# Transposed planes joined behind a later gate in every Strassen pair, and the third row's weight sums loaded sooner through a larger ring

## The chip, the cores and the metric

The kernel runs on one core of a Trainium2 chip. The metric is the device time of one execution in microseconds (us). The engines of the core are TensorE (PE in the profile), VectorE (DVE), ScalarE (ACT) and GpSimd (POOL); SyncE (SP) issues all transfers, in order.

## The reference

Eight heads of banded attention over 8 batches of 576 positions, then a gated feed-forward layer over the 4608 tokens, in float32.

```python
rel = pos[:, None] - pos[None, :]
mask = (rel >= 0) & (rel < 64)
scores = np.where(mask, scale * q @ k.T, -1e9)
attn = softmax(scores);  x = attn @ v          # 4608 x 512 after the heads are joined
gate = 1.0 / (1.0 + np.exp(-(x @ w_gate)))     # 512 -> 1536
val = x @ w_val
return (gate * val @ w_out).astype(np.float32) # 1536 -> 512
```

## The kernel before

The 4608 tokens are 12 tiles of 384. Every float32 product of the feed-forward layer is three matmuls: each operand is split into a high part, cast to fp32r on ACT, and the rest, a subtraction on DVE.

Tiles 0 and 1 go through the layer plainly (`up`, `down`). Tiles 2 to 11 go in five pairs, s = 1 to 5, each as a two by two block product by the Strassen-Winograd scheme, with seven block products instead of eight. A pair has 6 values of k, each with 7 products for the gate (m = 0) and 7 for the value (m = 1); these are the matmuls `pr` of L668. Then it has 7 times 6 last products, the matmuls `y`, also of L668. A "step" below is one pair of `pr` products, or one last product. The products of a k give, in turn, `u` and `c` (sums on DVE), `g` (tanh on ACT, L450) and `h` (DVE, L455), and `h` is summed (L621 to L643) and split (L750, L751) for the last products.

Pairs 2 to 5 use weight blocks and sums of blocks (`wd`, `wod`) that pair 1's phase puts into DRAM. For the up projections POOL makes the sums S1 to S4 (`sums_make`, L589 to L595) from the plain float32 weights: `sums_load` brings two rows `a` of `w32d` for each k and m, POOL makes the sums `sw`, and `sums_split` splits them into the weights `ws` of pair 1 (L602 on ACT, L604 on DVE for m = 1, L609 on POOL for m = 0). The rows `a` of k = 0 have tiles of their own, those of k = 1 share one tile of the ring `raw` (6 buffers of 4 KB a partition), those of k = 2 and later take two buffers of the ring `w32` (3 buffers of 2 KB a partition). The ring `w32` also holds `yo` (outputs of tiles 0 and 1 on their way to DRAM), `t1` (a sum of x blocks) and planes `pl`, below. DVE makes the sums of the down weights from `wa` (`wo_sums`, L553 to L561).

The attention of a pair is done while the pair before it is in the layer. For each unit (tile t, pair of heads p) PE makes the scores, DVE and ACT the exponentials `p` (two halves, h = 0 and 1), then `p` must be transposed before it meets `v`. Units before tile 4, and some of tiles 4 and 5, are transposed by PE (`stage_b`: `pp`, L347, and a copy on ACT, L352). The others go by the transfers: `stage_d` copies `p` on ACT into two 16-bit planes `pl` (L368), and SP issues a transposing transfer into `plT` (L374); `stage_e` joins the planes back into `p` on ACT (L383). Then PE makes the outputs (`outputs`, L406), and ACT copies them to `xf`, from which DVE makes the next pair's x sums.

The order on the engines comes from a list of events with a time each (`put`), sorted, and then from a scheduler of the framework that orders every engine but PE by a simulation; PE keeps the written order. `visit(("u", i), stage, ...)` places an attention stage behind step i of the up products, `visit(("d", i), ...)` behind last product i. In each pair three visits (v = 1 to 3 at steps u = 5, 19, 33) take two units each, c and d. `tc.issue_after(marks["gate"])` puts an instruction behind the latest tanh `g`, `marks["cast"]` behind the latest cast of L750, and `chain[-1]` behind the latest exponential.

SP's transfers use eight semaphores in turn, so a transfer also waits until the one eight places earlier has landed. In the orders below `DMAHW`*n* is that semaphore.

Of the kernel before, what the change touches and what calls it, by code (L numbers as in the profile page):

```python
# [27 lines left out]
def attn_ffn(ctx: ExitStack, tc: tile.TileContext, qT, kT, vN, w_gate, w_val, w_out, out, outT):  # L28
# [18 lines left out]
    RAW, W32 = 6, 3  # L47
# [4 lines left out]
    mp = ctx.enter_context(tc.tile_pool(name="mp", bufs=2))  # L52
# [30 lines left out]
    marks = {"pT": {}}  # L83
    chain = []
# [273 lines left out]
    def stage_d(t, p, last, home=None, base=6):  # L358


        for h in range(2):
            halves = st[(t, p, h)].rearrange("p u c -> p (u c)").bitcast(U16).rearrange("p (n e) -> p e n", e=2)
            pool, tag, bufs = home or ((mp, "g", 4) if last else (mp, "w32", W32))
            if tag[0] == "e":
                tag = f"e{EXTRA - 2 + h}"
            pl = pool.tile([P, 2, TT], U16, name=f"pl{h}_{t}_{p}", tag=tag, bufs=bufs)
            with tc.issue_after(marks["cast"]) if last and not home else nullcontext():
                nc.scalar.copy(pl, halves)  # L368
            if last:
                plT = ap.tile([P, 2 * UP, P], U16, name=f"plT{h}_{t}_{p}", tag=last, bufs=2)  # L370
            else:
                ft, fp = unit(t // 2, base + h)
                plT = xp.tile([P, 2 * UP, P], U16, name=f"plT{h}_{t}_{p}", tag=f"xf{4 * (ft % 2) + fp}")
            nc.sync.dma_start_transpose(out=plT, in_=pl.rearrange("p e n -> p (e n)"))  # L374
            turned_of[(t, p, h)] = plT

    def stage_e(t, p, last=False):
        for h in range(2):
            halves = st[(t, p, h)].rearrange("p u c -> p (u c)").bitcast(U16).rearrange("p (n e) -> p n e", e=2)
            plT = turned_of.pop((t, p, h))  # L380
            mark = chain[-1] if t < 6 else marks["cast"] if last else marks["gate"] if h else None
            with tc.issue_after(mark) if mark else nullcontext():
                nc.scalar.copy(halves, plT.rearrange("p (e u) c -> p (u c) e", e=2))  # L383

    turned_of = {}
# [182 lines left out]
    def sums_load(m, k):  # L568
        aa = []
        for i in range(2):  # L570
            if (m, k) in EARLY:
                a = xp.tile([P, DM], F32, name=f"a{i}_{m}_{k}", tag=f"x{EARLY[m, k] + i}")
            elif k == 1:
                if i == 0:
                    both = mp.tile([P, 2, DM], F32, name=f"a_{m}_{k}", tag="raw", bufs=RAW)
                a = both[:, i, :]
            else:
                a = mp.tile([P, DM], F32, name=f"a{i}_{m}_{k}", tag="w32", bufs=W32)
            nc.sync.dma_start(out=a, in_=w32d[m][k + i * NK])
            aa.append(a)  # L580
        sums[m, k] = aa
# [208 lines left out]
    def put(tm, o, f, *a):  # L790
        events.append((tm, o, f, a))

    AHEAD = 2
    DPT = DNT / TB
    APT = (0.9, 0.8, 0.9, 1.5, 0, 2.7, 0, 0, 1.6)
    stages = (stage_a, stage_b, stage_c, stage_s, stage_n, stage_v, stage_d, stage_e, stage_o)
    LOAD_AHEAD = 8
    BEFORE, BEHIND = 0, 12
# [9 lines left out]
    for n in range(2 * NP):  # L808
        t, p = divmod(n, NP)
# [6 lines left out]
    def unit(s, n):  # L816
        return 2 * s + n // 2 % 2, n // 4 + n % 2 * 2
# [9 lines left out]
    at, now = {}, 0.0  # L827
    MERGED = (0, 1, 2, 3)
    for n, (x, y, z) in enumerate(((4.5, 7.5, 8.5), (9, 12, 13), (13.5, 16, 17), (17.5, 20.5, 22), (22.5, 25, 26), (26.5, 30, 31), (31.5, 35, 36), (36.5, 40, 41))):
        u = unit(1, n)  # L830
# [20 lines left out]
    for i, (kind, t, j) in enumerate(plan):  # L851
        attend(i)
        at[(kind, t, j)] = now
        if (kind, t, j) == ("up", 0, 0):
            now = -9.9 - UPT / 2
# [10 lines left out]
        if (kind, t, j) == ("up", 0, 0):  # L866
            now = 0.0
    for i in range(KINDS * NF):
        j, m = divmod(i, KINDS)
# [37 lines left out]
        put(now + load, 7, wo_sums_load, k)  # L907
        put(now + make, 7, wo_sums, k)
    DOUBLE = (5, 19, 33)
    LAST_OUT, FIRST_IN = 6, 9  # L910
    for s in range(1, NS):
        fill.clear()

        def visit(key, *what):
            fill.setdefault(key, []).append(what)

        if s + 1 < NS:
            for v, u in enumerate(DOUBLE, 1):
                c, d = new = [unit(s + 1, 2 * v + i) for i in range(2)]
                visit(("u", u), 5, new, [unit(s + 1, 2 * v - 2 + i) for i in range(2)])  # L920
                visit(("u", u + 1.5), 4, *d)
                visit(("u", u + 2.5), 4, *c)
                home = (xp, "e", 1) if s == 1 and v < 3 else None
                visit(("u", u + 2.5), 6, *d, None, home)
                visit(("u", u + 6), 7, *d)
                if s == 1 and v < 3:
                    visit(("u", u + 7), 1, *c)
                elif s == 1 and v == 3:
                    visit(("u", u + 6), 1, *c)
                elif v < 3:  # L930
                    visit(("u", u + 4.5), 6, *c, None, home, 4)
                    visit(("u", u + 8.5), 7, *c)
                else:
                    visit(("u", u + 4.5), 6, *c, "k", (mp, "w32", W32))
                    visit(("d", 1), 7, *c, True)
            if s + 2 == NS:
                visit(("d", LAST_OUT), 8, c, d)
        if 1 <= s < NS - 2:
# [9 lines left out]
        for k in range(NK):  # L948
            if s == 1:
                for m in range(2):  # L950
                    make = (-28 + 7 * m, -29 + 6 * m)[k] if k < 2 else -25 + 8 * m
                    put(now + make - 6, 7, sums_load, m, k)
                    put(now + make, 7, sums_make, m, k)
                    for i, at_cut in zip((0, 2), (-14 + 2 * m, -10 + 2 * m) if k == 0 else (-13 + 1.5 * m, -5 + 1.5 * m)):
                        put(now + at_cut, 7, sums_split, m, k, i)
                        put(now + at_cut + 4, 7, sums_store, m, k, i)
                for n, d in ((0, -23 if k == 0 else -14), (4, -12 if k == 0 else -4), (5, -9 if k == 0 else -1)):
                    put(now + d, 7.5, w_load, s, k, n)
            else:
                for n in range(NPR):  # L960
                    put(now - 22 + 2.1 * n, 7.5, w_load, s, k, n)
            for n in range(NPR):
                for m in range(2):
                    put(now, 9, product, s, k, n, m)
                    now += PRT
                    if m == 0:
                        attend(("u", NPR * k + n - 0.5))
                attend(("u", NPR * k + n))
            put(now + 0.5, 5, h_prep, s, k)
            if k < EXTRA:  # L970
                put(now + 3, 5.1, h_early, s, k)
# [46 lines left out]
    for tm, _, f, a in events:  # L1018
        if f in (conv_a, conv_b, conv_c):
            with ExitStack() as behind:  # L1020
# [4 lines left out]
                j, m = divmod(a[0], KINDS)  # L1025
# [56 lines left out]
```

## Time and profile before

| | |
|---|---|
| three runs | 927.86, 931.34, 931.66 us, median 931.34 |
| profiled execution | 930.14 us, span 928.4 us |
| PE busy | 909.9 us, 98% of the span, 7002 matmuls |
| DVE, ACT, POOL busy | 711.2 (77%), 552.4 (59%), 154.2 (17%) us |
| TensorE clock granted | 1.00 over the span |

The span reaches from the first instruction to the last; the time of the execution is 1.7 us longer. PE is busy nearly everywhere, so the time moves only by what makes PE wait, or no longer wait.

### The profile page before, as it was taken

The numbers are of one execution on the slowest core, as the hardware profiler recorded it, in microseconds if no ns is written. First come the engines' busy times: TensorE is split into PE (matmuls) and PEld (weight loads), VectorE is DVE, ScalarE is ACT, GpSimd is POOL, SyncE is SP. The second block draws the span as 40 slices with busy tenths as digits, with TensorE's granted clock in tenths as the row PEclk, the third lists the DMA queues.
The fourth block names the chain that finished last, engine by engine and source line by source line (L and its number), as shares of the span: only waits on it lengthen the run. The fifth ranks groups of instructions, "written<-read, shape, count | busy, mean of one in ns | idle before, by whom it ended". The sixth has DMA issues, their size and how long they took to land.

```text
span 928.4 us, 20123 instructions
## 1 busy us (share of the span) xinstructions
PE 909.9 (98%) x7002; PEld 878.1 (95%) x7002; DVE 711.2 (77%) x1919; ACT 552.4 (59%) x1414; POOL 154.2 (17%) x232
## 2 busy tenths in 40 slices
PE   6999999999999999999999999999999999999998
PEld 4799999889999999999999999999999999999998
DVE  7999989889788995676896666897566797566882
ACT  7866766566565774653975545886446575222450
POOL 4210103803766010110110101100101100000000
PEclk9999999999999999999999999999999999999999
DMA  9899988989999999999989999989999898988374
GB/s 335 309 390 367 357 306 294 347 281 362 342 351 357 370 348 388 312 308 288 297 272 353 319 306 319 253 314 306 370 288 324 244 275 282 288 254 260 117 227 160
DMA packets 148710, 284.07 MB, mean 306 GB/s; under 512 B 54656, under 2 KB 76800, under 8 KB 148608
## 3 DMA queue, kind: packets, MB, share of 16 engines
q1 hardware_dynamic: 148608, 282.78, 92.3%
q8 instruction: 56, 0.92, 0.4%
q14 instruction: 46, 0.38, 0.1%
HBM read 220.20 MB, written 51.90 MB: 293 GB/s over the span
## 4 chain that ended last, share of the span: by engine, by line
PE 77%; DVE 8%; DMA 7%; ACT 3%; issue 2%; POOL 1%; SPq 0%; DVEq 0%; ACTq 0%; POOLq 0%
PE pr L668 40%; PE y L668 24%; PE ph L442 5%; PE y L490 2%; DMA a<-w32d 2%; PE pr L406 2%; ACT p L259 1%; DMA plT<-pl 1%; DMA wa<-w32d 1%; DVE w L160 1%; DVE p L251 1%; PE pp L347 1%; DMA raw<-in_moe_w_val_dram 1%; PE pr L226 1%; DMA wt<-wd 1%
## 5 line engine op out<-in xcount | busy, mean ns | idle before, releaser
L668 PE MATMUL pr<-x_T,wt 128*128 128x384 f32 x1224 | 222.0, 335 | 1.2 <-DVE u L678 0.6
L668 PE MATMUL y<-h,wot 128*128 128x384 f32 x1260 | 220.4, 335 | 0.0
L668 PEld LDWEIGHTS y<-h,wot 128*128 128x128 f32 x1260 | 218.4, 188 | 0.6 <-issue 0.5
L668 PEld LDWEIGHTS pr<-x_T,wt 128*128 128x128 f32 x1224 | 212.7, 188 | 2.5 <-DVE u L678 1.5
L668 PE MATMUL pr<-x_B,wt 128*128 128x384 f32 x1008 | 186.3, 336 | 0.0
L668 PEld LDWEIGHTS pr<-x_B,wt 128*128 128x128 f32 x1008 | 175.4, 188 | 1.6 <-issue 1.5
L276 POOL TENSOR_TENSOR p<-p,rs 128x384 f32<-128x384 f32 x76 | 71.9, 959 | 522.4 <-DVE rs L267 335.5
L751 DVE TENSOR_TENSOR h<-h,h 128x384 fp32r<-128x384 f32 x210 | 111.0, 569 | 26.4 <-ACT h L750 26.1
L750 ACT CAST h<-h 128x384 fp32r<-128x384 f32 x210 | 101.1, 512 | 50.4 <-DVE h L455 19.7
L259 ACT ACTIVATE p<-p,mn 128x128 f32<-128x128 f32 x288 | 110.6, 391 | 12.1 <-DVE mn L251 10.8
L450 ACT ACTIVATE g<-c 128x384 f32<-128x384 f32 x90 | 47.0, 523 | 107.7 <-DVE c L707 101.3
L442 PE MATMUL ph<-x,w 128*128 128x384 f32 x576 | 106.1, 339 | 0.5 <-DVE h L455 0.5
L442 PEld LDWEIGHTS ph<-x,w 128*128 128x128 f32 x576 | 99.8, 188 | 3.4 <-DVE h L455 0.9
L383 ACT COPY p<-plT 128x768 uint16<-128x768 uint16 x54 | 49.0, 923 | 21.5 <-DMA plT<-pl 21.4
L678 DVE TENSOR_TENSOR c<-pr,p 128x384 f32<-128x384 f32 x60 | 33.1, 551 | 37.0 <-PE pr L668 37.0
L455 DVE SCALAR_TENSOR_TENSOR h<-g,c 128x384 f32<-128x384 f32 x90 | 50.3, 559 | 11.0 <-ACT g L450 5.0
L368 ACT COPY pl<-p 128x768 uint16<-128x768 uint16 x54 | 43.8, 833 | 18.2 <-DMA plT<-pl 15.0
L259 ACT ACTIVATION_READ_ACCUMULATOR p<-p,mn 128x1 f32 x264 | 49.6, 188 | 0.0
L683 ACT COPY p<-pr 128x384 f32<-128x384 f32 x60 | 27.7, 473 | 28.2 <-PE pr L668 28.1
L678 DVE TENSOR_TENSOR u<-pr,p 128x384 f32<-128x384 f32 x60 | 32.4, 550 | 15.7 <-PE pr L668 15.6
L668 PE MATMUL pr<-x_T,ws 128*128 128x384 f32 x216 | 39.6, 337 | 1.5 <-DVE u L678 1.5
L668 PEld LDWEIGHTS pr<-x_T,ws 128*128 128x128 f32 x216 | 37.4, 188 | 2.3 <-DVE u L678 2.2
(256 smaller groups left out, 1221.0 us busy)
## 6 DMA issues: line engine op xcount, KB each, us to landing
wt<-wd SPq DMA_DIRECT2D x186, 512.0 KB, 4.8
wot<-wod SPq DMA_DIRECT2D x105, 512.0 KB, 5.1
v<-in_vN_dram SPq DMA_DIRECT2D x48, 384.0 KB, 5.3
wd<-ws SPq DMA_DIRECT2D x48, 256.0 KB, 5.1
k<-in_kT_dram SPq DMA_DIRECT2D x48, 224.0 KB, 5.5
q<-in_qT_dram SPq DMA_DIRECT2D x48, 192.0 KB, 5.5
w32d<-w SPq DMA_DIRECT2D x36, 256.0 KB, 5.2
wd<-w SPq DMA_DIRECT2D x36, 256.0 KB, 5.5
```

Source lines behind the costliest of these rows:

```text
L259: exp = nc.scalar.activation(pt[:, u, :], pt[:, u, :], AF.Exp, bias=mn[:, u:u + 1], scale=-1.0, **sums)
L276: eng.tensor_mul(out=pt, in0=pt, in1=rs.unsqueeze(2).broadcast_to([P, UP, P]))
L368: nc.scalar.copy(pl, halves)
L383: nc.scalar.copy(halves, plT.rearrange("p (e u) c -> p (u c) e", e=2))
L442: pe(nc.tensor.matmul(ph, l, r, start=i == 0, stop=i == len(prs) - 1))
L450: act = nc.scalar.activation(g, c, AF.Tanh)
L455: nc.vector.scalar_tensor_tensor(out=out, in0=g, scalar=1.0, in1=val, op0=ALU.add, op1=ALU.mult)
L668: pe(nc.tensor.matmul(ps, l, r, start=first and i == 0, stop=last and i == 2, skip_group_check=not check))
L678: marks["plus"] = nc.vector.tensor_add(out=o, in0=ps, in1=a).ins
L683: nc.scalar.copy(st["p1"], ps)
L750: marks["cast"] = nc.scalar.copy(h2[:, 0, :], src).ins
L751: nc.vector.tensor_sub(out=h2[:, 1, :], in0=src, in1=h2[:, 0, :].bitcast(F32))
```

## The change

The three parts of the diff are these. (1) `stage_d` and `stage_e` always put their copies behind a mark: the latest cast where `last` is set, else the latest tanh. (2) The visits of d's joins move from u + 6 to u + 7; in pairs 2 to 4 c's planes move from u + 4.5 to u + 7.5 and its joins from u + 8.5 to u + 11.5. In the third visit c's planes leave the tag "k" and take the ring `w32` and `xf` tiles as the others, and its joins move from last product 1 to last product 4. `LAST_OUT`, where the last attention outputs of all stand (pair 4), moves from last product 6 to 9. (3) The rows `a` of k = 2 share one buffer of `raw`, as those of k = 1, and the loads of k = 2 and later stand 9 instead of 6 time units ahead of their sums. One line is gone, so the lines behind L381 count one less in the changed kernel.

```diff
@@ stage_d
-            with tc.issue_after(marks["cast"]) if last and not home else nullcontext():
+            with tc.issue_after(marks["cast" if last else "gate"]):
                 nc.scalar.copy(pl, halves)
@@ stage_e
-            mark = chain[-1] if t < 6 else marks["cast"] if last else marks["gate"] if h else None
-            with tc.issue_after(mark) if mark else nullcontext():
+            with tc.issue_after(marks["cast" if last else "gate"]):
                 nc.scalar.copy(halves, plT.rearrange("p (e u) c -> p (u c) e", e=2))
@@ sums_load
-            elif k == 1:
+            elif k in (1, 2):
                 if i == 0:
                     both = mp.tile([P, 2, DM], F32, name=f"a_{m}_{k}", tag="raw", bufs=RAW)
                 a = both[:, i, :]
@@ the pairs
-    LAST_OUT, FIRST_IN = 6, 9
+    LAST_OUT, FIRST_IN = 9, 9
@@ visits of c and d
                 home = (xp, "e", 1) if s == 1 and v < 3 else None
                 visit(("u", u + 2.5), 6, *d, None, home)
-                visit(("u", u + 6), 7, *d)
-                if s == 1 and v < 3:
-                    visit(("u", u + 7), 1, *c)
-                elif s == 1 and v == 3:
-                    visit(("u", u + 6), 1, *c)
-                elif v < 3:
-                    visit(("u", u + 4.5), 6, *c, None, home, 4)
-                    visit(("u", u + 8.5), 7, *c)
-                else:
-                    visit(("u", u + 4.5), 6, *c, "k", (mp, "w32", W32))
-                    visit(("d", 1), 7, *c, True)
+                visit(("u", u + 7), 7, *d)
+                if s == 1:
+                    visit(("u", u + (7 if v < 3 else 6)), 1, *c)
+                    continue
+                visit(("u", u + 7.5), 6, *c, None, home, 4 if v < 3 else 6)
+                visit(("u", u + 11.5) if v < 3 else ("d", 4), 7, *c)
@@ sums of the weights, pair 1
-                    put(now + make - 6, 7, sums_load, m, k)
+                    put(now + make - (9 if k > 1 else 6), 7, sums_load, m, k)
```

PE's order is the same in both kernels, but for 18 matmuls of last products that stand ahead of the outputs of pair 4 instead of behind them. The other engines' orders move in many places; three follow.

SP, while tiles 0 and 1 end (a block of weight 5 for k = 0, the first outputs `yo`, attention inputs). Before:

```order
L516 DMA wt_1_0_5_3040<-wd_0_5_154 128x1024 [waits DMAHW0_49,PE_49]
L494 DMA out_0_dram<-yo_0_0_2690 128x512 [waits DMAHW1_49,Activation_49]
L529 DMA wd_0_3_152<-ws2_1_0_3067 128x512 [waits DMAHW2_49,DVE_49]
L494 DMA out_0_dram<-yo_0_1_2696 128x512 [waits DMAHW3_49,Activation_49]
L494 DMA out_0_dram<-yo_0_2_2702 128x512 [waits DMAHW4_49,Activation_49]
L193 DMA v_4_0_3007<-in_vN_dram 128x768 [waits DMAHW5_49,PE_49]
L529 DMA wd_0_6_155<-ws2_1_0_3067 128x512 [waits DMAHW6_49]
L182 DMA q_4_2_2809<-in_qT_dram 128x384 [waits DMAHW7_49,PE_49]
```

and with the change:

```order
L578 DMA a_0_2_3158<-w32d_0_2_115 128x512 [waits DMAHW0_49]
L578 DMA a_0_2_3158<-w32d_0_8_121 128x512 [waits DMAHW1_49]
L515 DMA wt_1_0_5_3040<-wd_0_5_154 128x1024 [waits DMAHW2_49,PE_49]
L578 DMA a_1_2_3266<-w32d_1_2_127 128x512 [waits DMAHW3_49,Pool_49]
L578 DMA a_1_2_3266<-w32d_1_8_133 128x512 [waits DMAHW4_49]
L493 DMA out_0_dram<-yo_0_0_2690 128x512 [waits DMAHW5_49,Activation_49]
L528 DMA wd_0_3_152<-ws2_1_0_3067 128x512 [waits DMAHW6_49,DVE_49]
L493 DMA out_0_dram<-yo_0_1_2696 128x512 [waits DMAHW7_49,Activation_49]
L493 DMA out_0_dram<-yo_0_2_2702 128x512 [waits DMAHW0_49,Activation_49]
```

The rows of k = 2 for the gate (`a_0_2`) and for the value (`a_1_2`) now stand ahead of the first `yo`; the second pair of them waits for POOL. That is the end of the sums of k = 1, m = 1 (`sw_1_1`).

DVE, some microseconds later, with the x sums of pair 1 (`t1`, `xf`, `x_T`) and the last unit of tile 3 (`p0_3_3`, `p1_3_3`, its normalisation L276). Before, with `t1_1_0` and `t1_1_1` higher up, at rows not shown, ahead of the exponentials of that unit:

```order
L663 TENSOR_TENSOR x_T2_1_0_2857<-xf_2_0_1307,x_T2_1_0_2857 128x384 [waits Activation_49]
L663 TENSOR_TENSOR x_T1_1_1_3074<-t1_1_1_3001,x_T1_1_1_3074 128x384 [waits Activation_49]
L266 SCALAR_TENSOR_TENSOR rs_3_3_2736<-rs_3_3_2736 128x3 [waits Activation_49]
L632 TENSOR_TENSOR xf_2_0_1307<-xf_2_2_1534,xf_2_0_1307 128x384 [waits DVE_49]
L267 RECIPROCAL rs_3_3_2736<-rs_3_3_2736 128x3 [waits DVE_49]
L266 SCALAR_TENSOR_TENSOR rs_3_3_2736<-rs_3_3_2736 128x3 [waits Activation_49]
L276 TENSOR_TENSOR p0_3_3_2734<-p0_3_3_2734,rs_3_3_2736 128x384 [waits DVE_49]
L267 RECIPROCAL rs_3_3_2736<-rs_3_3_2736 128x3 [waits DVE_49]
L663 TENSOR_TENSOR x_T4_1_0_2912<-xf_2_0_1307,x_T4_1_0_2912 128x384 [waits Activation_49]
L276 TENSOR_TENSOR p1_3_3_2746<-p1_3_3_2746,rs_3_3_2736 128x384 [waits DVE_49]
```

and with the change, from `t1_1_0` on (two rows further down stands `p1_3_3`'s L276, behind one more x sum):

```order
L620 TENSOR_TENSOR t1_1_0_2829<-xf_3_0_1775,xf_2_0_1307 128x384 [waits DMAHW5_49,DMAHW0_49,Activation_49]
L266 SCALAR_TENSOR_TENSOR rs_3_3_2736<-rs_3_3_2736 128x3 [waits Activation_49]
L620 TENSOR_TENSOR t1_1_1_3001<-xf_3_1_2718,xf_2_1_2239 128x384 [waits DMAHW7_49,DMAHW2_49]
L621 TENSOR_TENSOR xf_3_0_1775<-xf_3_2_2032,xf_3_0_1775 128x384 [waits DVE_49]
L628 TENSOR_TENSOR xf_2_0_1307<-xf_3_2_2032,t1_1_0_2829 128x384
L267 RECIPROCAL rs_3_3_2736<-rs_3_3_2736 128x3 [waits DVE_49]
L266 SCALAR_TENSOR_TENSOR rs_3_3_2736<-rs_3_3_2736 128x3 [waits Activation_49]
L662 TENSOR_TENSOR x_T1_1_0_2878<-t1_1_0_2829,x_T1_1_0_2878 128x384 [waits Activation_49]
L276 TENSOR_TENSOR p0_3_3_2734<-p0_3_3_2734,rs_3_3_2736 128x384 [waits DVE_49]
L267 RECIPROCAL rs_3_3_2736<-rs_3_3_2736 128x3 [waits DVE_49]
L662 TENSOR_TENSOR x_T1_1_1_3074<-t1_1_1_3001,x_T1_1_1_3074 128x384 [waits Activation_49]
L662 TENSOR_TENSOR x_T3_1_0_2890<-xf_3_0_1775,x_T3_1_0_2890 128x384 [waits Activation_49]
```

Both `t1` now stand between the exponentials and the normalisation of `p0_3_3` and `p1_3_3`, and each waits for a `yo` to have left its `w32` buffer (DMAHW5 is the first `yo` above, DMAHW7 the second).

ACT, at the end of the up products of pair 2 (unit 1 of tile 7 is c of the third visit, unit 3 is d). Before:

```order
L450 ACTIVATE g_4_11_6586<-c5_0_2_5_6584 128x384 [waits DVE_49]
L750 CAST h_3_2_0_6636<-h_2_0_5423 128x384 [waits PE_49]
L750 CAST h_3_2_1_6657<-h_2_1_5692 128x384 [waits PE_49]
L383 COPY p0_7_1_6398<-plT0_7_1_6530 128x768 [waits DMAHW0_49,Activation_49]
L383 COPY p1_7_1_6407<-plT1_7_1_6534 128x768 [waits DMAHW2_49,Activation_49]
L750 CAST h_3_2_2_6670<-h1_2_2_5852 128x384 [waits PE_49]
L450 ACTIVATE g_5_5_6611<-c6_0_2_5_6609 128x384 [waits DVE_49]
L750 CAST h_3_2_3_6687<-h0_2_3_6126 128x384 [waits PE_49]
L750 CAST h_3_2_4_6698<-h0_2_4_6287 128x384 [waits PE_49]
L683 COPY p1_y0_2_6704<-y0_0_2_6628 128x384 [waits PE_49]
L683 COPY p1_y1_2_6709<-y0_1_2_6632 128x384 [waits PE_49]
```

and with the change:

```order
L749 CAST h_3_2_1_6655<-h_2_1_5682 128x384 [waits PE_49]
L449 ACTIVATE g_5_5_6601<-c6_0_2_5_6599 128x384 [waits DVE_49]
L368 COPY pl0_7_1_6609<-p0_7_1_6396 128x768 [waits Pool_49]
L368 COPY pl1_7_1_6613<-p1_7_1_6405 128x768 [waits Pool_49]
L749 CAST h_3_2_2_6666<-h1_2_2_5850 128x384 [waits PE_49]
L749 CAST h_3_2_3_6683<-h0_2_3_6116 128x384 [waits PE_49]
L749 CAST h_3_2_4_6694<-h0_2_4_6285 128x384 [waits PE_49]
L382 COPY p0_7_1_6396<-plT0_7_1_6611 128x768 [waits DMAHW0_49,Activation_49]
L682 COPY p1_y0_2_6702<-y0_0_2_6626 128x384 [waits PE_49]
L682 COPY p1_y1_2_6707<-y0_1_2_6630 128x384 [waits PE_49]
L749 CAST h_4_2_0_6722<-h_2_0_5421 128x384 [waits DVE_49]
L382 COPY p1_7_1_6405<-plT1_7_1_6615 128x768 [waits DMAHW1_49,Activation_49]
```

Before, c's planes `pl0_7_1`, `pl1_7_1` stood 18 and more rows ahead of `g_5_5`, and its joins ahead of it too. Now the planes stand behind `g_5_5`, the joins some rows later, the second behind the copies `p1_y`. SP has the two transposes of c right behind the load of `wot_2_7` now; before they stood 7 and 5 rows ahead of it.

## Rows read from the trace of the kernel before

**Rows 1.** Busy time by stretch; per engine busy us (count), PEclk, DMA share, GB/s.

```profile
0.00:40.00 40.00, 28.90 (x450) 23.11 (x452) 31.67 (x160) 31.61 (x106) 16.45 (x28) 1.00 0.91 338
160.00:300.00 140.00, 137.09 (x1116) 126.60 (x1116) 117.14 (x333) 85.91 (x236) 74.00 (x136) 1.00 0.99 339
300.00:920.00 620.00, 619.38 (x4537) 612.19 (x4536) 451.62 (x1145) 349.15 (x859) 45.36 (x48) 1.00 0.92 294
```

**Rows 2.** PE's waits over the span: total us, times, longest us.

```profile
PE s L226 <- DMA k<-in_kT_dram: 4.9, 2, 4.0
```

**Rows 3.** PE's timeline at four places: start us, us, what, idle before and its releaser.

```profile
190.82 1.13 PE L347 MATMUL pp<-ident,p 128*128 128x128 f32 x6
...
253.65 2.37 PE L668 MATMUL pr<-x_T,ws 128*128 128x384 f32 x12 [1.38 <-DVE u L678]
...
276.46 1.86 PE L668 MATMUL pr<-x_T,wt 128*128 128x384 f32 x9 [0.55 <-DVE c L678]
...
577.55 2.38 PE L668 MATMUL pr<-x_T,wt 128*128 128x384 f32 x12 [0.60 <-DVE u L678]
```

**Rows 4.** ACT's timeline ahead of two of those places.

```profile
247.39 0.93 ACT L383 COPY p<-plT 128x768 uint16<-128x768 uint16 x1 [1.08 <-DMA plT<-pl]
...
570.70 0.93 ACT L383 COPY p<-plT 128x768 uint16<-128x768 uint16 x1 [2.56 <-DMA plT<-pl]
```

**Rows 5.** POOL's timeline, 177 to 273 us.

```profile
182.09 1.30 POOL L595 TENSOR_TENSOR sw<-a,sw 128x128 f32<-128x128 f32 x2
...
218.90 2.61 POOL L609 TENSOR_TENSOR ws<-sw,ws 128x128 fp32r<-128x128 f32 x4 [35.51 <-ACT ws L602]
...
271.28 1.28 POOL L589 TENSOR_TENSOR sw<-a 128x128 f32<-128x128 f32 x2 [6.36 <-DMA a<-w32d]
```

**Rows 6.** SP's queue, 176 to 198 us: issue time, us it took.

```profile
179.54 0.34 SPq L494 DMA_DIRECT2D out_dram<-yo  x1
```

**Rows 7.** Landing of the three `yo` stores of 170 to 200 us.

```profile
DMA to landing us min/median/max: 2.7/2.8/4.2
```

**Rows 8.** DVE's timeline, 180 to 219 us, and at 456 us.

```profile
180.19 0.76 DVE L663 TENSOR_TENSOR x_B<-xf,x_B 128x384 fp32r<-128x384 f32 x1
...
183.84 0.56 DVE L621 TENSOR_TENSOR t<-xf,xf 128x384 f32<-128x384 f32 x1 [0.77 <-DMA out_dram<-yo]
...
185.37 0.55 DVE L663 TENSOR_TENSOR x_T<-t,x_T 128x384 fp32r<-128x384 f32 x1
...
190.74 0.55 DVE L276 TENSOR_TENSOR p<-p,rs 128x384 f32<-128x384 f32 x1
...
206.16 0.42 DVE L553 TENSOR_TENSOR wb<-wa 128x256 f32<-128x256 f32 x1 [2.33 <-DMA wa<-w32d]
...
217.57 0.55 DVE L678 TENSOR_TENSOR u<-pr,p 128x384 f32<-128x384 f32 x1
...
455.77 0.56 DVE L621 TENSOR_TENSOR t<-xf,xf 128x384 f32<-128x384 f32 x1 [1.45 <-DMA plT<-pl]
```

**Rows 9.** PE's timeline around the first last products of pair 2.

```profile
458.85 10.56 PE L668 MATMUL y<-h,wot 128*128 128x384 f32 x60
...
469.34 0.92 PE L406 MATMUL o_(8, 0)_6756<-p,v 128*64 128x64 f32 x24
```

**Rows 10.** ACT's timeline there.

```profile
452.08 0.83 ACT L368 COPY pl<-p 128x768 uint16<-128x768 uint16 x1 [0.22 <-DMA plT<-pl]
...
462.95 0.52 ACT L450 ACTIVATE g<-c 128x384 f32<-128x384 f32 x1
...
464.76 1.00 ACT L683 COPY p_y<-y 128x384 f32<-128x384 f32 x2 [0.47 <-PE y L668]
```

**Rows 11.** SP's queue there.

```profile
450.33 2.67 SPq L374 DMA_TRANSPOSE plT<-pl  x2
...
461.12 0.32 SPq L523 DMA_DIRECT2D wot<-wod  x1
```

**Rows 12.** Landing of `plT`, all 54 transposes.

```profile
DMA to landing us min/median/max: 2.9/4.7/9.8
```

## The prediction

> **What bounds the kernel now.** I read busy time by stretch first [rows 1]. PE is busy for 137.09 of the 140 us from 160 to 300, and for 619.38 of the 620 us from 300 to 920. No engine's order differs before 178 us, so the 11.1 us in which PE idles in the first 40 stay. The matmuls are the same 7002. What the change can take away is therefore the idle time behind 160: 2.91 + 0.62 = 3.5 us. The measurement tells about 0.5% from no change, 4.65 us; a clear gain would need more than all of that idle time. A loss has no such bound, so most of the work below looks for new waits.
>
> Next I read PE's timeline for the waits themselves [rows 3]: 1.38 us at 253.65 for a sum `u`, 0.55 at 276.46 for `c`, 0.60 at 577.55 for `u`, and none ahead of the transposes `pp` at 190.82. Then, for each, the engine behind it [rows 4, 5].
>
> **What the change takes away.** Ahead of 253.65, ACT stood 1.08 us at 247.39 in a join that waited for its plane, with the tanh and the weights' cast queued behind it [rows 4]. With the join behind a tanh and one step later the plane has landed. I count half of the wait, 0.65, since the splits of `ws` on that path remain; the ends are 0 and 1.38. Ahead of 276.46, POOL idled 6.36 us for rows `a` [rows 5], and ACT's cast and DVE's split of `ws` followed late. POOL is otherwise idle from 183.39 to 218.90 (35.51 us, rows 5 again), and the loads now bring the sums of k = 2 into that gap and the later ones a k earlier: −0.55. Ahead of 577.55 a join of ACT waited 2.56 us [rows 4]; moved behind the tanh it no longer holds up that chain: −0.60. Together −1.8, with ends 0 and −2.53.
>
> DVE's stop of 1.45 us at 455.77 for a plane [rows 8] goes too, as that x sum now stands further back. PE did not wait there, so this is worth nothing by itself; it lets ACT's tanh come sooner, which I use below.
>
> **What it adds near 191 us.** SP works in order. The load `a_1_2` now stands ahead of the first `yo` and waits for POOL's last sum of k = 1, which starts at 182.09 and takes 1.30: 183.39 [rows 5]. Before, that `yo` was issued at 179.54, each such issue taking 0.34 [rows 6]. Now two loads go out first, so it leaves at about 184.2, and the second `yo`, two issues on, at 184.9. The stores landed 2.7 to 4.2 us after issue [rows 7]: 187.6 to 189.1 for the second.
>
> DVE's `t1_1_0` and `t1_1_1` each need a `w32` buffer that a `yo` frees. Before, `t1_1_0` already waited 0.77 us for it and ran at 183.84 [rows 8]. Both now stand ahead of the normalisation of `p0_3_3` and `p1_3_3`. From the start of `t1_1_1` to the end of the second normalisation there are nine operations over 128x384: `t1_1_1`, two `xf`, `x_T1`, L276, three `x_T`, L276. One takes 0.55 us alone (185.37) and 0.76 while POOL works (180.19) [rows 8], and POOL will be making the sums of k = 2 here. So 5.0 to 6.8 us, ending at 192.6 to 195.9. Before, the second normalisation ended at 190.74 + 0.55 = 191.29. PE's order is fixed, and the last products of tile 1 are queued behind the transposes `pp`, so PE stands: 1.3 to 4.6 us. With the middle of the landing (3.45) and 0.65 an operation it is 184.9 + 3.45 + 5.9 − 191.29 = **+3.0**.
>
> DVE then carries this on, with two operations more moved behind the normalisation (1.1 us). Its sums of the down weights end right at the first `u` at 217.57, and 2.33 us of idle time for `wa` at 206.16 lie between [rows 8]. That idle time hides the 1.1 if the `wa` do not come later too; their loads stand behind the same SP queue. Between 0 and 1.1 I take **+0.5**. The other moved transfers (attention inputs and the rows `a` of later k) go at nothing: SP has gaps there and their users run many steps later. If that cover failed, the price would be an `a` wait as the 0.55 above.
>
> **What it adds at the third visit.** The outputs of c, which PE makes at 469.34, 10.5 us behind the first last product at 458.85 [rows 9], need both joins of c. ACT's planes for them now stand behind the last tanh of the pair, which ran at 462.95 [rows 10]. Without DVE's stop of 1.45 and with ACT's earlier planes gone I put it at 460.7 to 461.5; each plane takes 0.83 (452.08, rows 10). SP, free once the load at 461.12 is out, issues one transpose in 1.33 us (two in 2.67) [rows 11]: the first at about 462.0, the second at 463.3. Landing takes 2.9 us at best, 4.7 in the median [rows 12]. At 4.7 the first plane is there at 466.7; then ACT does a join (0.93, rows 4), two copies `p_y` (1.00, rows 10), a cast (taken as one such copy, 0.5) and the second join (0.93), ending at 470.0. PE waits 0.7. At 3.6 us it would wait nothing. I take 0.45 for each of pairs 2, 3 and 4, whose orders are alike here (in pair 4 the outputs move to the same place by `LAST_OUT`): **+1.4**, with ends 0 and 3.3 (1.1 each, with the tanh late).
>
> `LAST_OUT` itself only swaps 18 matmuls with the outputs, nothing. The joins of visits 1 and 2 have several steps before their outputs, nothing.
>
> **The sum** is 3.0 + 0.5 − 1.8 + 1.4 = +3.1 on the profiled execution's 930.14 (span 928.4 and 1.7 around it): 933.2. That execution lies 1.2 below the median of the three runs, 931.34, from which it would be 934.4. I say **933.5**.
>
> [...]
>
> **The rivals.**
> - *Joins late (0.24).* The third visit's planes land late three times. Each us beyond the middle case costs 3 in all. It decides from a landing of about 5.6 us, where PE waits 1.4 at each: the sum becomes +5.9, 936 and more; at 6.3 us of landing 938. For it: the longest landing is 9.8 [rows 12], and a load of weights goes out just ahead of the two. Against: the median of 4.7.
> - *Only the savings (0.15).* POOL ends sooner, or the scheduler's order leaves DVE enough room, and the stop at 191 stays under 1 us, the joins without a wait: 930.14 − 1.8 + 0.5, about 929. Against it: the wait of 0.77 that `t1_1_0` had already with the `yo` issued 4.7 us earlier.
> - *All idle time goes (0.07).* The moved loads and joins clear every wait behind 160: 930.14 − 3.5 = 926.6, just over the bound for faster. Against it: the new orders on SP and DVE above.
> [...]
>
> My forecast, the stop at 191 with small waits at the joins, has 0.50; its own range is 930.5 to 936. The range that leaves out no more than 2 in 10 takes in the savings and the late joins: 928 to 939. Faster by over 0.5% (below 926.7) 0.07; slower (above 936.0) 0.24 for the joins, 0.03 of the clock and 0.04 of the forecast's upper end, 0.31; within, 0.62.
>
> **What would show it.** For the stop at 191: in SP's queue the first `yo` at about 184 instead of 179.54, a DVE `t` at 187 to 189 waiting for it, and a PE wait of 1 to 5 us at `pp` for L276 of DVE. For the savings: no PE wait at the places of 276.46 and 577.55, less than 1.38 at that of 253.65, and POOL busy between 184 and 195. For the joins: PE waits at the three outputs (in this trace 469.34), for ACT's join, of 0 to 1.1 us each. The forecast is wrong if `pp` shows no wait, if a join wait passes 1.4, if PE waits over 1 us at a place not named here, or if the granted clock falls below 1.00.

## The result and the profile after

The changed kernel takes 934.67 us in the median of six runs (934.08 to 936.81), the kernel before 930.91 in six: a ratio of 1.0052 (1.0038 to 1.0066). It is slower, by an amount that lies across the 0.5% bound of the prediction. The profiled execution took 934.58 us, span 932.7, 4.4 more than that of before.

PE's waits over the span of the changed kernel (total us, times, longest us):

```profile
PE s L226 <- DMA k<-in_kT_dram: 4.9, 2, 3.9
...
PE o L405 <- ACT p L382: 1.7, 1, 1.7
PE pp L347 <- DVE rs L267: 1.5, 1, 1.5
PE pp L347 <- DVE p L276: 1.4, 1, 1.4
PE pr L667 <- DVE u L677: 0.9, 2, 0.6
...
PE o_(10, 0)_8661 L405 <- ACT p L382: 0.3, 1, 0.3
```

The two `pp` waits are the forecast stop at 191. The two `o` waits are joins of the third visit, in pairs 3 and 4. The `u` waits are the places of 217 and 253; those at 276.46 and 577.55 are gone. By stretch (columns as in [rows 1]):

```profile
0.00:40.00 40.00, 30.73 (x452) 24.71 (x454) 31.68 (x160) 31.67 (x106) 16.45 (x28) 1.00 0.91 338
160.00:300.00 140.00, 135.87 (x1100) 124.74 (x1099) 116.19 (x309) 83.47 (x222) 76.68 (x136) 0.99 0.96 331
300.00:920.00 620.00, 617.95 (x4527) 611.31 (x4528) 454.52 (x1165) 350.67 (x873) 45.35 (x48) 1.00 0.93 295
```

Beside [rows 1], PE lost 1.2 us of busy time from 160 to 300 and 1.4 behind it. The granted clock reads 0.99 in the second stretch, and that is the line to follow. SP's queue at 182 us (start, us it took):

```profile
182.22 0.80 SPq L578 DMA_DIRECT2D a<-w32d  x2
183.11 0.38 SPq L493 DMA_DIRECT2D out_dram<-yo  x1
...
184.06 1.32 SPq L493 DMA_DIRECT2D out_dram<-yo  x2
```

DVE's timeline behind it (start, us, operation, idle time before it and its releaser):

```profile
186.69 0.62 DVE L620 TENSOR_TENSOR t<-xf,xf 128x384 f32<-128x384 f32 x1 [3.52 <-DMA out_dram<-yo]
...
187.95 0.56 DVE L620 TENSOR_TENSOR t<-xf,xf 128x384 f32<-128x384 f32 x1 [0.29 <-DMA out_dram<-yo]
188.43 0.82 DVE L621 TENSOR_TENSOR xf<-xf,xf 128x384 f32<-128x384 f32 x1
...
190.72 0.80 DVE L276 TENSOR_TENSOR p<-p,rs 128x384 f32<-128x384 f32 x1
...
192.91 0.54 DVE L276 TENSOR_TENSOR p<-p,rs 128x384 f32<-128x384 f32 x1
```

PE's timeline there:

```profile
191.66 0.52 PE L347 MATMUL pp<-ident,p 128*128 128x128 f32 x3 [1.49 <-DVE rs L267]
193.60 0.87 PE L347 MATMUL pp<-ident,p 128*128 128x128 f32 x3 [1.42 <-DVE p L276]
194.12 3.50 PE L489 MATMUL y<-w,h 128*128 128x512 f32 x9
197.55 0.92 PE L405 MATMUL oo<-p,v 128*64 128x64 f32 x24
```

The chain reads from one fence to the next. The first `yo` leaves at 183.11 instead of 179.54 [rows 6]. DVE stands 3.52 us for it, so both normalisations come late, and PE stands twice, 1.49 + 1.42 = 2.91 us. POOL worked until 191.10. Beside it some of DVE's operations took 0.80 to 0.82, others 0.55 to 0.62; behind it they took 0.52 to 0.55.

Then look at the durations, not the waits. Three `pp` take 0.52 us in the first line and 0.87 in the second. Nine `y` take 3.50; in the kernel before the same nine took 2.30:

```profile
181.70 0.88 PE L226 MATMUL s<-k,q 64*64 64x128 f32 x22 [0.22 <-ACT xf L394]
...
191.71 2.30 PE L490 MATMUL y<-w,h 128*128 128x512 f32 x9
193.94 0.92 PE L406 MATMUL oo<-p,v 128*64 128x64 f32 x24
```

The windows of 2 us say why (PE busy is the second number, the granted clock the third from the end):

```profile
190.00:192.00 2.00, 0.51 (x4) 0.31 (x3) 2.00 (x7) 0.93 (x2) 1.10 (x2) 1.00 1.05 385
192.00:194.00 2.00, 0.58 (x4) 0.43 (x3) 2.00 (x6) 0.04 (x1) 0.00 (x0) 0.81 0.86 330
194.00:196.00 2.00, 2.00 (x8) 1.61 (x7) 2.00 (x6) 1.66 (x4) 0.00 (x0) 0.50 0.06 22
196.00:198.00 2.00, 2.00 (x20) 1.45 (x20) 1.97 (x6) 1.42 (x3) 0.00 (x0) 0.84 0.00 0
198.00:200.00 2.00, 2.00 (x24) 1.67 (x20) 2.00 (x5) 1.52 (x3) 0.00 (x0) 1.00 0.66 136
```

PE did 0.51 and 0.58 us of work in 4 us. From 194 to 196 the granted clock is 0.50 while PE is busy throughout; at 198 it is 1.00 again. The cost is (0.87 − 0.52) + (3.50 − 2.30) = 1.55 us that no list of waits shows. The places of the matmuls agree: those that ran at 181.70 in the kernel before run at 180.90, 0.8 sooner (most of it at 173.11, ahead of every difference in order: the kernel before waits 0.48 us there for `h`, the changed one does not), and the `oo` of 193.94 at 197.55, 3.6 later. That is 4.4 us lost in between, beside 2.91 + 1.55 = 4.46.

ACT's timeline at the joins of the third visit, pair 2 and pair 4:

```profile
469.22 0.93 ACT L382 COPY p<-plT 128x768 uint16<-128x768 uint16 x1 [2.75 <-DMA plT<-pl]
...
759.81 0.93 ACT L382 COPY p<-plT 128x768 uint16<-128x768 uint16 x1 [4.35 <-DMA plT<-pl]
...
761.80 0.92 ACT L382 COPY p<-plT 128x768 uint16<-128x768 uint16 x1
```

PE's timeline at the last attention outputs, pair 4:

```profile
762.87 1.58 PE L405 MATMUL o<-p,v 128*64 128x64 f32 x46 [1.66 <-ACT p L382]
```

In pair 2 the plane came soon enough and PE did not wait. In pair 4 ACT stood 4.35 us, and the second join ended at 762.72, just ahead of the outputs.

### The profile page after: what moved, and what is told of

The parts are those of the page before. It is cut to its first block, busy times and chain, and to the rows that moved or that the text cites. A ratio compares the mean times of both kernels' runs of the same rounds, so it can differ in the third digit from the quotient of the medians.

```text
span 932.7 us, 20103 instructions
## 1 busy us (share of the span) xinstructions
PE 913.5 (98%) x7002; PEld 881.3 (94%) x7002; DVE 715.4 (77%) x1919; ACT 551.8 (59%) x1414; POOL 156.9 (17%) x232
## 4 chain that ended last, share of the span: by engine, by line
PE 84%; DVE 5%; ACT 4%; DMA 3%; issue 1%; SPq 0%; POOL 0%; DVEq 0%; ACTq 0%; POOLq 0%
PE pr L667 45%; PE y L667 21%; PE ph L441 8%; PE y L489 2%; PE pr L405 2%; DMA plT<-pl 1%; PE pp L347 1%; ACT p L259 1%; PE pr L226 1%; DMA raw<-in_moe_w_val_dram 1%; ACT p L382 1%; DVE p L251 1%; PE s L226 1%; DMA wa<-w32d 1%; ACT h L749 1%
## 5 line engine op out<-in xcount | busy, mean ns | idle before, releaser
L276 POOL TENSOR_TENSOR p<-p,rs 128x384 f32<-128x384 f32 x76 | 71.9, 959 | 520.9 <-DVE rs L267 392.4
```

Source lines behind the costliest of these rows:

```text
L276: eng.tensor_mul(out=pt, in0=pt, in1=rs.unsqueeze(2).broadcast_to([P, UP, P]))
```

## The experiments

The theory: the time is lost at 191, because SP's order holds `yo` back, and at the third visit; the rest of the change gains a little. Its rivals: the clock, the moved loads wherever they stand, and the joins as the main loss. Ratios are to the kernel before on the same chip.

**Part 3 undone, and part 3 alone.** The first keeps the joins and visits; the second puts only this into the kernel before:

```diff
-            elif k == 1:
+            elif k in (1, 2):
-                    put(now + make - 6, 7, sums_load, m, k)
+                    put(now + make - (9 if k > 1 else 6), 7, sums_load, m, k)
```

> Parts 1 and 2 alone: the rows of k = 2 stay in the small ring and are loaded at their old lead. Late-stores theory (the loss is the stop of PE at the transposes near 191 us, 2.9 us of wait and about 1.5 us of a lower clock, both made by the moved loads): no PE wait of DVE's L276 there, the clock 1.00 in every stretch, the wait of about 0.55 us near 276 us back, a join wait of 1 to 2 us in pair 4; time 930.9 - 1.4 + 2.0 = about 931.5, ratio 1.000 to the kernel before. Rival (the loss comes from the joins and planes put behind tanh and moved later): the loss stays, 934 to 935, ratio 1.003 to 1.005.

> Part 3 alone: the rows of k = 2 in the large ring, loads at lead 9, joins and planes as before. Late-stores theory: first store of yo near 183, PE waits of about 2.9 us in all at the transposes near 191, granted clock about 0.9 in the stretch 180 to 200, no wait near 276; time 930.9 + 4.4 - 0.6 = 934.7, ratio 1.004. Rival (the joins make the loss): 930 to 931, ratio 1.000 or below.

Joins alone: 931.83 us, 1.0013 (1.0001 to 1.0025). Its profiled execution was its longest, 934.73; in it PE waited 2.30 us for `u` at 255.48, where the kernel before waits 1.38, and the clock fell behind it, to 0.50 from 258 to 260, which was not expected. Sums alone: 935.20 us, 1.0053 (1.0033 to 1.0074), with waits at `pp` of 1.20 and 1.88 us and the clock at 0.50 behind them:

```profile
194.78 0.60 PE L347 MATMUL pp<-ident,p 128*128 128x128 f32 x3 [1.88 <-DVE p L276]
195.06 3.90 PE L490 MATMUL y<-w,h 128*128 128x512 f32 x9
```

```profile
196.00:198.00 2.00, 2.00 (x6) 1.58 (x5) 1.97 (x6) 1.61 (x4) 0.00 (x0) 0.50 0.00 0
```

So the sums carry the loss, and they alone make the stop.

**Only the second pair of loads back at a lead of 6.** Its order puts `a_1_2` behind all three `yo`.

```diff
-                    put(now + make - (9 if k > 1 else 6), 7, sums_load, m, k)
+                    put(now + make - (9 if k > 2 or k == 2 and m == 0 else 6), 7, sums_load, m, k)
```

> The changed kernel with one load moved back: the rows of k = 2 for the value (a_1_2) at lead 6, so that they stand behind the three yo stores; all else as changed. Late-stores theory: the first yo leaves near 179, no PE wait over 0.5 us at the transposes near 191, clock 1.00; time 934.7 - 4.4 = 930.3, ratio 0.999 to the kernel before. Rival (POOL's sums of k = 2 slow DVE there, whatever the stores do): POOL's sums run at almost the same time, so a wait of 1 us or more stays, 932 or more.

This missed: 934.25 us, 1.0036 (1.0022 to 1.005). The `yo` left at 179.07, as before, but this is their landing:

```profile
DMA to landing us min/median/max: 5.6/5.7/5.8
```

And these are DVE's timeline and, below it, PE's, in the same run:

```profile
184.94 0.56 DVE L620 TENSOR_TENSOR t<-xf,xf 128x384 f32<-128x384 f32 x1 [3.71 <-DMA out_dram<-yo]
...
191.24 1.53 DVE L276 TENSOR_TENSOR p<-p,rs 128x384 f32<-128x384 f32 x2
```

```profile
192.19 0.52 PE L347 MATMUL pp<-ident,p 128*128 128x128 f32 x3 [2.37 <-DVE p L276]
```

The stores landed in 5.6 to 5.8 us instead of the 2.7 to 4.2 of [rows 7], so `t` started at 184.94 instead of 183.84 [rows 8], 1.10 later. Beside POOL's sums the two normalisations then took 1.53 us and ended at 192.77 instead of 191.29, 1.48 later; and PE came to the place 1.0 us sooner than in the kernel before (189.82 against 190.82). The place in the queue is thus not the whole cause. That the loads of k = 2 delay the landing is not shown: in this run other transfers of those microseconds landed late too (`wt` in 7.0 us against 4.7), but in the changed kernel, where two such loads go out 0.9 us ahead of the first `yo`, the stores landed in 3.5 to 3.9 us. The clock read 1.00 in all windows from 186 to 202, behind a wait of 2.37.

**The third visit as early as before.** All else as in the change.

```diff
-                visit(("u", u + 7.5), 6, *c, None, home, 4 if v < 3 else 6)
-                visit(("u", u + 11.5) if v < 3 else ("d", 4), 7, *c)
+                visit(("u", u + (7.5 if v < 3 else 4.5)), 6, *c, None, home, 4 if v < 3 else 6)
+                visit(("u", u + 11.5) if v < 3 else ("d", 1), 7, *c)
```

> The changed kernel with the third visit back at its old places (planes at u + 4.5, joins behind last product 1; the tags as changed). Late-stores theory: the stop near 191 stays with its clock of about 0.9, the join waits of pairs 3 and 4 (0.3 and 1.7 us, and a few tenths of single matmuls) go; 934.7 - 2.1 = 932.6, ratio 1.002 to before. Rival (the joins are the loss): 930.5 to 931.5, ratio 1.000.

931.89 us, 1.0015 (1.0004 to 1.0027), with the stop at 191 still there (1.82 and 1.42, clock 0.57). No join made PE wait. That is 0.37%, some 3.4 us, below the ratio of the changed kernel.

**The loads of k = 2 behind those of `wa`.** SP's and DVE's orders at 191 are then those of before.

```diff
-            nc.sync.dma_start(out=a[:, i, :], in_=w32d[2][k + i * NK])
+            marks["wa"] = nc.sync.dma_start(out=a[:, i, :], in_=w32d[2][k + i * NK]).ins
-            nc.sync.dma_start(out=a, in_=w32d[m][k + i * NK])
+            with tc.issue_after(marks["wa"]) if k == 2 else nullcontext():
+                nc.sync.dma_start(out=a, in_=w32d[m][k + i * NK])
```

> The changed kernel with the loads of k = 2 queued on SP behind those of wa_2, which puts SP, DVE and POOL near 191 us back into the order of the kernel before and keeps the sums of k = 2 in POOL's gap (about 205 to 215). Theory now (the stop near 191 is made by the loads standing in front there: later stores, stores that land late, and DVE's order with the x sums ahead of the normalisation): no PE wait over 0.3 us there, no wait near 276, the join waits of pairs 2 to 4 stay at about 2 us; time 930.1 - 0.6 - 0.7 - 0.6 + 2.1 = 930.3, ratio 1.000. Rival (POOL's earlier work slows DVE wherever it lies, and the loss moves on to the first u near 218): a wait of 1 us or more near 218, 933 or more.

> The same with the third visit at its old places. Theory: both costs gone, the savings of waits near 276 and 577 (and part of 253) left: 930.1 - 1.5 = 928.6, ratio 0.998 to 0.999. Rival (the waits that go come back later, or the clock decides): 930 to 931, ratio 1.000.

The first gave 933.15 us, 1.0038 (1.0024 to 1.0053), as its rival had it; the second, with the early third visit, 931.43 us, 1.0017 (1.0005 to 1.0029), also nearer its rival. The stop at 191 had gone (0.25 us was left), but a new one stood at the first `u`. SP's queue in the first of the two runs:

```profile
200.97 1.60 SPq L579 DMA_DIRECT2D a<-w32d  x3
...
207.62 2.79 SPq L543 DMA_DIRECT2D wa<-w32d  x5
```

PE's timeline behind it, then the window with the granted clock:

```profile
220.81 1.43 PE L668 MATMUL pr<-x_T,ws 128*128 128x384 f32 x6 [3.59 <-DVE u L678]
```

```profile
222.00:224.00 2.00, 2.00 (x10) 1.96 (x9) 2.00 (x5) 1.71 (x4) 1.66 (x1) 0.50 1.05 399
```

The rows `a` now stand ahead of the later `wa`, and DVE's sums of the down weights, queued ahead of `u`, come late. Two things are mixed in that: DVE waits 1.04 us for `wa` at 212.56, and from 207.74 to 217.80 it works beside POOL's sums of k = 2, where POOL idled before [rows 5]; DVE's splits of 128x512 there take up to 0.95 us, 0.68 behind it. No run takes the two apart. The clock falls behind this wait too, and behind that of 3.24 us at the same place in the second run: it reads 0.50 from 222 to 224 in both. The loads moved the stop 30 us on.

**A stop of known length, nothing else changed.** Into the kernel before, behind the last normalisation, DVE does two or four operations more that leave the values as they are:

```diff
+        if (t, p, h) == (3, NP - 1, 1):
+            for _ in range(2):
+                nc.vector.scalar_tensor_tensor(out=pt, in0=pt, scalar=0.0, in1=pt, op0=ALU.mult, op1=ALU.add)
```

> The kernel before with two added operations of DVE on p1_3_3 behind its normalisation (p + 0 * p, the same values), so that PE stops at the transposes near 191 for about 1.4 us in one piece. If a stop costs only its own length: 930.1 + 1.4 = 931.5, granted clock 1.00 in 190 to 200. If a stop of any length here lets the clock fall: the clock under 1.00 there and 1 us or more on top, 932.5 or more.

> The same with four added operations: PE stops for about 4 us. If a stop costs only its own length: 930.1 + 4 = 934, clock 1.00 in 190 to 200. If it also lets the clock fall, as in the changed kernel: a stretch at 0.50 behind it, 1.5 to 2 us on top, 936.

Two operations: 932.38 us, 1.0026 (1.0013 to 1.0039). Four: 934.64, 1.0047 (1.003 to 1.0063). PE's timelines, two first, four second:

```profile
192.78 0.52 PE L350 MATMUL pp<-ident,p 128*128 128x128 f32 x3 [1.53 <-DVE p L279]
193.06 2.29 PE L493 MATMUL y<-w,h 128*128 128x512 f32 x9
```

```profile
195.73 0.88 PE L350 MATMUL pp<-ident,p 128*128 128x128 f32 x3 [4.63 <-DVE p L279]
196.26 3.57 PE L493 MATMUL y<-w,h 128*128 128x512 f32 x9
```

Behind 1.53 us the same nine matmuls take 2.29, behind 4.63 us 3.57: the long stop pays (0.88 − 0.52) + (3.57 − 2.29) = 1.6 us more than its own length. The short stop's 932.38 us are near its second case, 932.5, though the clock reads 1.00 behind it; two waits of 0.47 us that the kernel before lacks (216.01 and 243.81) are a part of the rest of its 2.4 us. The long one shows the fall of the clock (0.50 from 196 to 198), but its time is near that of the case without, 934: of 4.63 + 1.6 = 6.2 us lost at 191, 4.4 are left by the ratio. Waits that PE had further on shrink behind the stop: 0.66 us at the place of 253.65, none at that of 577.55. So a stop with a fall of the clock, and nothing else of the change, can cost as much as the change does (1.0047 beside 1.0052); it does not show that the change has no other loss.

**The loads behind the attention's keys of tile 5, with the third visit early, and with it as in the change.** Both start `a_0_2` at a lead of 2.

```diff
-            nc.sync.dma_start(out=kt, in_=kT[rows, c0:c0 + TT + BLK])
+            kd = nc.sync.dma_start(out=kt, in_=kT[rows, c0:c0 + TT + BLK])
+        if t == 5:
+            marks["k5"] = kd.ins
-            nc.sync.dma_start(out=a, in_=w32d[m][k + i * NK])
+            with tc.issue_after(marks["k5"]) if k == 2 else nullcontext():
+                nc.sync.dma_start(out=a, in_=w32d[m][k + i * NK])
-                    put(now + make - (9 if k > 1 else 6), 7, sums_load, m, k)
+                    put(now + make - (2 if (m, k) == (0, 2) else 9 if k > 1 else 6), 7, sums_load, m, k)
```

> As the last but one pair of kernels (loads of k = 2 later on SP, third visit at its old places), but the loads of k = 2 stand behind the keys of tile 5, past the rows wa_3 and wa_4 for which DVE waited. Theory (each place in SP's queue takes the time of what stands behind it): no wait at 191, the wait of 3.2 us at the first u near 219 falls to 1 us or less; 931.4 - 2.5 = 929, ratio 0.998 to 1.000. Rival (POOL's sums of k = 2, now from 211 to 220, slow DVE's sums of the down weights, which end at that u): a wait of 1.5 to 3 us there, 930.5 to 932.

> The loads of k = 2 behind the keys of tile 5, with the third visit left as the change has it: what its later planes and joins cost where nothing stops PE near 191. Theory: the waits for ACT's joins come back, 0.3 to 0.7 us in pairs 2 and 3 and about 1.7 in pair 4, 2.2 in all; ratio 0.9955 + 0.0024 = 0.998 to before, about 929. Rival (the late joins cost more than PE's waits for them show, as between the changed kernel and the one with only its third visit early, 3.4 us by their ratios): 0.999 to 1.000, 930 to 931.

With the early third visit 926.48 us, **0.9955 (0.9937 to 0.9972)**: faster than both kernels, and more than was expected. With that of the change 930.53, 0.9999 (0.9986 to 1.0012), as its rival had it; the last outputs wait 1.65 us for a join. In both profiled executions (930.57 and 929.29 us) PE still waits 1.76 us for the first `u`. That of the first, the longest of its six runs:

```profile
221.98 1.32 PE L670 MATMUL pr<-x_T,ws 128*128 128x384 f32 x6 [1.76 <-DVE u L680]
```

**Visits 1 and 2 alone, and `LAST_OUT`.** The first is the changed kernel with part 3 undone and the third visit early; the second is the fastest kernel so far with one line turned back:

```diff
-    LAST_OUT, FIRST_IN = 9, 9
+    LAST_OUT, FIRST_IN = 6, 9
```

> The gates and the later visits 1 and 2 alone: part 3 undone, third visit at its old places, LAST_OUT 9. Theory: no join waits, no wait near 577, the waits near 253 and 276 as before or a little changed; 930.1 - 0.6 = 929.5, ratio 0.999 to 1.000. Rival (the gate behind a tanh delays the weights' splits near 253, as the wait of 2.3 us there in the joins-only kernel could mean): a wait of 2 us or more at 253, 931 to 932, ratio 1.001.

> The fastest version so far (loads of k = 2 behind the keys of tile 5, third visit early) with LAST_OUT back at 6: the outputs of pair 4 stand three last products sooner, where the joins have less time. Theory: the joins behind last product 1 end before last product 6, so no wait and no difference: ratio 0.995 to 0.997, 926 to 928. Rival (the outputs then wait for the last join): a PE wait of 0.5 to 1.5 us for ACT's join in pair 4, ratio 0.996 to 0.998.

Visits 1 and 2 alone: 928.87 us, 0.9976 (0.9964 to 0.9988), below what was expected. With `LAST_OUT` 6: 926.38, 0.9965 (0.9948 to 0.9981), no difference from 0.9955 that can be told. What the loads behind the keys of tile 5 add to visits 1 and 2, 0.1 to 0.2%, is not clear of the intervals. In the profiled execution with `LAST_OUT` 6 (926.0 us) these are three of PE's waits, and below them the stretch behind 300:

```profile
PE s L228 <- DMA k<-in_kT_dram: 5.1, 2, 3.9
PE pp L349 <- POOL p L278: 2.2, 4, 0.7
...
PE pr L670 <- DMA wt<-wd: 0.5, 1, 0.5
```

```profile
300.00:920.00 620.00, 620.00 (x4544) 613.36 (x4543) 451.85 (x1139) 346.21 (x847) 45.23 (x48) 1.00 0.93 292
```

In this execution PE has no idle time left behind 300 us, and no wait for a join, for `u`, or for DVE at `pp` stands in the list. The same order of loads has the wait of 1.76 us in the executions above; POOL's and DVE's timelines show what differs. First the execution of 930.57 us, then this one:

```profile
213.92 1.40 POOL L591 TENSOR_TENSOR sw<-a 128x128 f32<-128x128 f32 x2 [30.24 <-DVE wb L555]
...
214.93 1.54 DVE L278 TENSOR_TENSOR p<-p,rs 128x384 f32<-128x384 f32 x2
```

```profile
211.12 5.52 POOL L591 TENSOR_TENSOR sw<-a 128x128 f32<-128x128 f32 x2 [29.47 <-DMA a<-w32d]
...
211.74 1.02 DVE L278 TENSOR_TENSOR p<-p,rs 128x384 f32<-128x384 f32 x2
```

In the first POOL's sums run at once and DVE's two normalisations take 1.54 us. In the second POOL's first two sums take 5.52 us, DVE's two normalisations beside them take 1.02, and its `u` is in time. (The profile's spans on POOL are rough; DVE's durations are the firmer sign.) So which of the two engines takes longer differs between these two executions; what decides it is not shown.

## Why the prediction was right, and where its sizes were off

The forecast case is what the trace shows: a stop at 191 of the size named, small waits at the joins, small savings. Its time was 1.2 us low. But two of the prediction's own signs of being wrong came too: a join wait passed 1.4 us, and the granted clock fell. Term by term, on the profiled pair:

| term | forecast | trace |
|---|---|---|
| stop at 191, its own length | +3.0 | 1.49 + 1.42 = 2.9 |
| clock behind it | 0 | 1.55 |
| DVE's carry to the first `u` | +0.5 | 0.5 |
| 253.65 | −0.65 | 0.61 − 1.38 = −0.77 |
| 276.46 and 577.55 | −1.15 | −1.15 |
| joins, third visit | +1.4 | 0 + 0.31 + 1.66 = 2.0 |
| sum | +3.1 | +5.0 |

The carry is read from the places of the matmuls, first the kernel before, then the changed one:

```profile
218.17 1.32 PE L668 MATMUL pr<-x_T,ws 128*128 128x384 f32 x6 [0.16 <-DVE u L678]
```

```profile
222.26 1.33 PE L667 MATMUL pr<-x_T,ws 128*128 128x384 f32 x6 [0.26 <-DVE u L677]
```

They lie 4.09 us apart, the `oo` of 197.55 and 193.94 3.61. Of these 0.5 us only 0.26 − 0.16 = 0.10 are a longer wait for `u`; most of the rest is lost at the `pp` just ahead. The spans differ by 4.3, and the changed kernel's execution was 0.8 ahead at 181: 5.1 us lost behind it, for a sum of 5.0. That the time came within 1.2 us is thus in part luck: the lead of 0.8, which no term of the forecast has, took back half of the clock's price.

- **The stop, right in place, in size partly by luck.** The steps came as written: `yo` at 183.11 (forecast 184), `t` at 186.69 and 187.95 waiting for it, PE at `pp`. The second normalisation ended at 193.45, 2.2 us later than before, where 3.0 was forecast; PE waited 2.9 because in this execution it came 0.65 sooner (190.17 against 190.82). The place in SP's queue, which the prediction has at the head of the chain, is not needed: with it restored the stores landed late and the stop came back, and with the loads behind `wa` it moved to the first `u`. What the loads cost is a matter of which work they stand beside. Behind tile 5's keys they cost 1.76 us at the first `u` in two profiled executions and nothing there in a third.
- **The clock, the term that was mis-sized.** The sum takes the stop at 191 at its own length, with nothing for the matmuls behind it. No run shows a stop of about 3 us there at that price: behind 1.49 + 1.42, 1.20 + 1.88 and 1.82 + 1.42 us the clock read 0.50 to 0.57, and in the changed kernel the matmuls behind the stop took 1.55 us longer; behind the shorter one of 2.37 it read 1.00. The wait of 4.0 us in [rows 2] is the one ahead of PE's first matmul, at 3.96, so it says nothing of a PE that was working. The chances leave the clock 0.03, for a time above 936.0; it fell, and the time was 934.67.
- **The savings, right in sum, in part not shown to come from the joins.** −1.9 against −1.8. POOL filled its gap from 182.26 to 191.1, as forecast, and no run with the loads sooner waits at 276.46, while the four with the old loads wait for `c` there or one step on, 0.36 to 0.98 us. The wait of 577.55 is gone with visits 1 and 2 alone, too. That of 253.65 is not settled: 0.65 us with visits 1 and 2 alone, 2.30 with joins alone, and 0.66 behind the long stop, which has nothing of the change.
- **The joins, in bounds in sum only.** Pair 2 had none; pair 4 had 1.66, above the 1.1 taken as the end for one pair and the 1.4 that was to count as wrong. Undoing the third visit alone gave as much as the 2.0 us of PE's waits or more: 0.37% in the change, 0.21% with the loads behind `wa`, 0.44% behind tile 5's keys, or 2.0 to 4.1 us. By the places of the matmuls the three pairs lost 0.15, 0.4 and 2.0 us in the changed kernel, 2.5 in all. Where the rest lies was not found.
- **"All idle time goes", 926.6.** Times of this size exist, in another order of the loads: medians of 926.4 and 926.5, with PE's idle time behind 300 us gone in one execution.

So the change mixes a gain and two losses: the gates with visits 1 and 2 (0.24% faster alone), the third visit (which takes that back: 1.0013 with it), and the loads, whose stop at 191 costs more than their savings.

## What to carry to other kernels

Before moving a load sooner, list what its queue and its neighbours in flight carry at the new place, and who waits for those; a gap of the engine that uses the load says nothing of that. Price a stop of TensorE by its length and by the matmuls behind it, and compare durations of equal groups of matmuls, since a list of waits does not show a lower clock (here 1.55 us, behind a stop of 2.91). Where a change has separable parts, time each one: here two of them cancelled, and the better order was found by keeping one and giving another a new place. Profile more than one execution of an order that looks good: with the loads behind tile 5's keys, the one of 926.0 us lacks a wait of 1.76 us that two others have.

## What the runs showed of the hardware

- **The clock fell behind some stops and not behind others.** It read 0.50 behind single waits of 4.63, 3.59 and 3.24 us, behind 1.49 + 1.42 with three matmuls between, and behind one of 2.30 at 255.48 in the run with the joins alone. It stayed at 1.00 behind 2.37, 1.76, 1.66 and 1.53. So 2.30 and 2.37 went opposite ways, and the length alone does not decide it in these traces. The two that I added up cost 1.55 and 1.6 us.
- **The mean clock of an execution varies by itself.** The kernel before was below 1.000 in 51 of 84 runs, and the runs below were no slower in the median than those at 1.000 on the same chip by more than 0.9 us. With the change it was below in all 6, with four operations in all 7, with two in 5 of 12, fewer than before. The mean clock alone therefore does not tell a kernel with a stop. The traces show one source, where the orders are alike: in 7 of the 14 profiled executions the 24 `oo` that start at 16 or at 21 us took 1.77 to 1.92 us, in the other 7 no more than 1.29. In six of the 7 the clock reads 0.91 or 0.92 over the 20 us around them, or 0.96 over the first 40; in the kernel before and the changed one it reads 1.00 there.
- **The same stores landed at very different speed**, all of 256 KB: in 2.7 to 4.2 us in the kernel before, 3.5 to 3.9 in the changed one, 5.6 to 5.8 in the run with the second pair of loads later. The cause was not isolated.
- **VectorE beside GpSimd.** Two-input operations over 128x384 took 0.52 to 0.56 us alone and, around 191 us, 0.55 to 0.82 while POOL made sums. It was not always VectorE that took longer: in the execution of 930.57 us two of POOL's sums took 1.40 us and VectorE's two normalisations 1.54, in that of 926.0 us the two sums took 5.52 and the normalisations 1.02. The cause was not isolated.
